# Routed attention and gated FFN on one core: q and k of six pairs cast over 128 partitions and moved by shifts, one output buffer less, a new order

## The chip, the cores and the metric

The kernel runs on one core of one Trainium2 chip. The time is the device time of one execution in microseconds (us); less is better. The kernel before was run three times: 248.41 us in the median, 248.40 to 248.58 from the fastest to the slowest.

A core has five engines that the text names as the profile does: PE (TensorE, matrix products, with its weight loads as PEld), DVE (VectorE), ACT (ScalarE), POOL (GpSimd) and SP (SyncE, which here only issues transfers). Each runs its own list of instructions strictly in order and waits where something it needs is not there yet.

## The reference, cut to what matters

```python
# q, k, v: 4 batches x 8 heads x 768 tokens x 64
q_assign = argmax(q_n @ c_n.T)               # nearest of 16 centroids, k likewise
mask = q_assign[:, :, :, None] == k_assign[:, :, None, :]
scores = where(mask, (q @ k.T) / 8, -1e9)
attn = exp(scores) / sum(exp(scores))
x = (attn @ v), heads side by side           # 4 x 768 x 512
h = relu(x @ w_in)                           # 512 -> 1024
conv = 3-tap filter along the tokens of h, per channel
out = (h * sigmoid(conv)) @ w_out            # 1024 -> 512
```

## The kernel before

**Work units.** Two heads of one batch are a pair; there are 16 pairs, 0 to 15, four per batch. For each pair the scores are made in the transposed form for half of the queries at a time, so there are 32 attention units t = 0 to 31: batch b = t // 8, half t % 8 // 4, pair 4b + t % 4. The feed-forward part has 8 units per batch (n = 0 to 31: two 128-channel blocks of the 1024, for half of the tokens).

**The path of a pair.** SP loads q, k and v (`load`, L243; `load_v`). Pairs 0 to 9 are transposed on PE (step T) and copied out of PSUM by DVE or ACT (Qd, Qa). Pairs 10 to 15 are loaded in 32x32 blocks by eight transfers (LQ.g.0 to .3, LK.g.0 to .3) and transposed in place on DVE (step D, `block_transpose`, L285). Both give `qkT`, a tile of 128 partitions (head 0 on partitions 0 to 63, head 1 on 64 to 127) by q and k. From it

- PE makes the similarities with the centroids (A, L302), DVE finds each token's centroid in seven steps M0 to M6 (L315) and packs it as three rows, PE turns them (K, L371), DVE or ACT copies them (Bd, Ba) and SP moves them into `ext` (BX, L381);
- q and k are cast to f16 into rows 0 to 63 of `ext`, one head at a time, in four instructions of 64x768 (CD with the engine's letter p, d or a, then the pair, head, and q or k; `cast_direct`, L288).

`ext` has five buffers, and holds q and k with the bias rows in rows 64 to 66, so that one product gives scores and mask together. v is cast by CV.

**Attention and the rest.** For each unit t: six score steps S.t.0 to S.t.5 (PE, L401), each followed by an exponential E (ACT, L413), values V (PE, L432), then NR and N on DVE (L443, L448: reciprocal of the sums, normalization). x is transposed by PE (X, with a copy Y) or by a transfer (XD), goes through I (PE, L486), a relu (Ra on ACT, Rd on DVE), filter taps on DVE (cw, aw, bw for whole units, c, a, b for halves, L518 and L520), tanh on ACT (H, L548) and the gate on DVE (G, L557). The output product is in steps O.b.tq.i of two matmuls each (L569); Fa or Fd copies a finished tile out of PSUM into `o_sb`, and FX stores it.

**What sets the order.** One string of steps, `PLAN`, is walked from left to right (`step`, L721) and each step appends its instructions to its engines' lists. Nothing reorders them later. `BUFS` gives the number of buffers of each rotating tile: writing into one whose last reader is not done makes the engine wait. Steps for another path of the casts are in the code, and no step of the order before calls them:

```python
def cast_direct(name, g, h, o):
    copy(name, ext_b[g % NE][0:D, h, o], qkT[g][D * h : D * (h + 1), o, :])

def cast_qk(name, g, o):
    if g not in c_t:
        c_t[g] = rot.tile([P, 2, S], F16, name="c16", tag="c16", bufs=BUFS["c16"])
    copy(name, c_t[g][:, o], qkT[g][:, o])

def shift_qk(g, h):
    nc.sync.dma_start(ext_b[g % NE][0:D, h], c_t[g][D * h : D * (h + 1)])
```

Of the kernel before, what the change touches and what calls it, by code (L numbers as in the profile page):

```python
# [19 lines left out]
BUFS = {'qk_in': 4, 'qkT': 2, 'c16': 2, 'v_in': 2, 'spk': 2, 'attn': 4, 'x16': 3, 'cnv': 2, 'th': 2, 'hg': 2, 'o_sb': 3, 'w_sb': 1, 'sim': 1, 'eqq': 1, 'val': 1, 'mx': 3, 'best': 3, 'rec': 3}  # L20

PLAN = (
# [123 lines left out]
def kernel(  # L146
# [91 lines left out]
    def qk_in(g):  # L238
        if g not in qk_t:
            qk_t[g] = rot.tile([P, 2, 2 * J * D], F32, name="qk_in", tag="qk_in", bufs=BUFS["qk_in"])  # L240
        return qk_t[g]
# [598 lines left out]
```

## Time and profile before

| | |
|---|---|
| median of 3 runs | 248.41 us |
| the profiled execution | 248.59 us |
| its span in the profile | 246.4 us |
| busy: PE, DVE, ACT, POOL | 232.0, 225.2, 212.7, 77.4 us |
| transfers | 32.07 MB, 130 GB/s in the mean |
| TensorE clock granted | 1.00 throughout |

The span reaches from the first to the last instruction of the program; 2.2 us of the execution lie around it. All durations are from this one execution. Matmuls are pipelined, so that one of 162 ns behind another shows as about 325 ns: PE's busy time says when PE has work, not that it works at its peak. An idle time is put down to what ended it.

### The profile page before, as it was taken

How to read it: one execution, taken by the hardware profiler on the slowest of the kernel's cores; microseconds unless marked ns; L12 is line 12 of the kernel's file. 1: busy time of each engine (PE TensorE's matmuls, PEld its weight loads, DVE VectorE, ACT ScalarE, POOL GpSimd, SP SyncE). 2: the span in 40 equal slices, each digit the busy share in tenths (PEclk: the TensorE clock that was granted, in tenths of full speed). 3: DMA queues.
4: the chain of work that ended last, by engine and by line, in shares of the span. 5: the costliest groups of instructions: out<-in, count | busy, mean ns of one | idle time of the engine just before them, and what ended most of it. 6: DMA issues, size and time to landing. Idle time of an engine off the chain costs nothing.

```text
span 246.4 us, 6267 instructions
## 1 busy us (share of the span) xinstructions
PE 232.0 (94%) x2447; PEld 148.2 (60%) x2447; DVE 225.2 (91%) x434; ACT 212.7 (86%) x331; POOL 77.4 (31%) x122
## 2 busy tenths in 40 slices
PE   8898999999999998798999999979999999999994
PEld 8675677666746674555455566645566666665541
DVE  6689867997999999999999999999999999999962
ACT  2578999997999999889899999979999999996730
POOL 6372681786162209346300615221500000000000
PEclk9999999999999999999999999999999999999999
DMA  8968999793480934646277984868300450002424
GB/s 160 220 158 212 262 211 327 217 287 83 124 193 13 203 56 82 126 80 122 45 131 159 232 74 122 153 86 135 84 19 6 124 182 0 3 1 109 150 85 170
DMA packets 95561, 32.07 MB, mean 130 GB/s; under 512 B 88361, under 2 KB 90921, under 8 KB 95532
## 3 DMA queue, kind: packets, MB, share of 16 engines
q1 hardware_dynamic: 93820, 31.25, 55.6%
q10 hardware_dynamic: 1712, 0.43, 1.0%
q8 instruction: 19, 0.31, 0.5%
q14 instruction: 10, 0.08, 0.1%
HBM read 23.11 MB, written 6.29 MB: 119 GB/s over the span
## 4 chain that ended last, share of the span: by engine, by line
PE 48%; DVE 33%; ACT 9%; issue 5%; DMA 3%; SPq 1%; POOL 0%; DVEq 0%; POOLq 0%; ACTq 0%
PE sc L401 13%; PE flex L569 9%; PE flex L432 7%; DVE cnv L520 6%; PE flex L486 5%; DVE hg L557 4%; PE flex L306 3%; ACT attn L413 3%; DMA xT<-x 3%; PE tail L569 3%; PE flex L278 3%; DVE eqq L339 3%; DVE x L448 2%; PE tail L486 2%; DVE cnv L518 2%
## 5 line engine op out<-in xcount | busy, mean ns | idle before, releaser
L413 ACT ACTIVATE attn<-sc 128x768 f16<-128x768 f32 x192 | 147.6, 830 | 6.2 <-PE sc L401 5.1
L401 PE MATMUL sc<-ext 128*128 128x384 f16 x384 | 90.8, 325 | 1.4 <-ACT attn L413 0.9
L236 POOL CAST ext<-qkT 64x768 f16<-64x768 f32 x44 | 44.0, 1008 | 72.4 <-DVE qkT L286 30.2
L520 DVE SCALAR_TENSOR_TENSOR cnv<-hpad,cwcol,cnv 128x768 f16<-128x768 f16 (+2 forms) x72 | 64.1, 904 | 0.2
L432 PEld LDWEIGHTS <-attn 128*128 128x128 f16 x1152 | 51.1, 97 | 18.7 <-issue 3.1
L432 PE MATMUL flex<-v,attn 128*128 128x65 f16 x1152 | 55.0, 193 | 0.1
L401 PEld LDWEIGHTS <-ext 128*128 128x128 f16 x384 | 31.6, 97 | 24.9 <-issue 10.9
L486 PE MATMUL flex<-xT,w_in 128*128 128x384 f16 x224 | 44.8, 325 | 1.0 <-DVE x L448 0.7
L569 PE MATMUL flex<-w_out,hg 128*128 128x512 f16 x160 | 43.7, 379 | 1.0 <-DVE x L448 1.0
L486 PEld LDWEIGHTS <-w_in 128*128 128x128 f16 x256 | 24.2, 97 | 17.1 <-issue 1.6
L557 DVE SCALAR_TENSOR_TENSOR hg<-th,hpad 128x768 f16<-128x768 f32 (+3 forms) x34 | 31.8, 944 | 0.5 <-ACT th L548 0.3
L548 ACT ACTIVATE th<-cnv 128x768 f32<-128x768 f16 (+2 forms) x30 | 26.1, 871 | 2.0 <-DVE cnv L520 1.8
L569 PEld LDWEIGHTS <-hg 128*128 128x128 f16 x192 | 17.5, 97 | 15.7 <-issue 1.4
L499 ACT ACTIVATE hpad<-flex 128x384 f16<-128x384 f32 x40 | 20.1, 518 | 0.2
L278 PE MATMUL flex<-id,qk_in 128*128 128x128 f32 x120 | 17.8, 277 | 1.9 <-DVE nrm_c L662 0.8
L448 DVE TENSOR_TENSOR x<-flex,rec 128x384 f16<-128x384 f32 x32 | 17.5, 546 | 0.5 <-DVE rec L443 0.3
L236 POOL CAST v<-v_in 128x768 f16<-128x768 f32 x12 | 11.3, 938 | 18.7 <-DMA v_in<-in_v_dram 10.4
L278 PEld LDWEIGHTS flex<-id,qk_in 128*128 128x128 f32 x120 | 13.5, 142 | 5.1 <-DVE nrm_c L662 1.0
L518 DVE TENSOR_SCALAR cnv<-hpad,cwcol 128x768 f16<-128x768 f16 (+2 forms) x36 | 15.4, 434 | 0.5 <-ACT hpad L499 0.3
L306 PE MATMUL flex<-qkT,cT 128*32 128x384 f32 x128 | 13.6, 498 | 0.5 <-DVE hpad L501 0.4
L234 ACT ACTIVATE qkT<-flex 128x512 f32<-128x512 f32 x15 | 8.8, 602 | 5.4 <-PE flex L278 5.4
L330 DVE STREAM_TRANSPOSE sim<-flex 128x384 f32<-128x384 f32 x16 | 9.2, 578 | 4.0 <-PE flex L306 3.6
(82 smaller groups left out, 223.1 us busy)
## 6 DMA issues: line engine op xcount, KB each, us to landing
v_in<-in_v_dram SPq DMA_DIRECT2D x16, 384.0 KB
out_dram<-o_sb SPq DMA_DIRECT2D x9, 512.0 KB
qk_in<-in_q_dram SPq DMA_DIRECT2D x20, 192.0 KB
qk_in<-in_k_dram SPq DMA_DIRECT2D x9, 384.0 KB
qk_in<-in_q_dram SPq DMA_DIRECT2D x24, 96.0 KB
qk_in<-in_k_dram SPq DMA_DIRECT2D x24, 96.0 KB
w_sb<-in_moe_w_in_dram SPq DMA_DIRECT2D x4, 512.0 KB
w_sb<-in_moe_w_out_dram SPq DMA_DIRECT2D x4, 512.0 KB
```

The source lines that it names most:

```text
L236: (nc.vector if name == "d" else nc.gpsimd).tensor_copy(out=to, in_=src)
L278: nc.tensor.transpose(bank[at][:, P * i : P * (i + 1)], qk_t[g][:, o, P * j : P * (j + 1)], id128[:])
L306: nc.tensor.matmul(bank[at][32 * j : 32 * (j + 1), 0:HS], lhsT=cT32[:, g % NPR, :], rhs=tokens[:, j], start=True, stop=True, skip_group_ch ...
L401: nc.tensor.matmul(s[:, n, 0:HS], lhsT=ext_b[g % NE][:, h, 1, P * (kt + n) : P * (kt + n + 1)], rhs=ext_b[g % NE][:, h, 0, HS * a : HS * ( ...
L413: nc.scalar.activation(attn[t, i // 3][:, kt : kt + 2, :], sc[(6 * t + i) % 2][:, :, 0:HS], AF.Exp, scale=0.125)
L432: nc.tensor.matmul(avp(at)[:, u, 0 : D + 1], lhsT=attn[t, h][:, kt, P * jq : P * (jq + 1)], rhs=v16_b[g % NE][:, h, kt, 0 : D + 1], start= ...
L448: nc.vector.tensor_tensor(out=x16[t].rearrange("p jq (h d) -> p h jq d", h=2), in0=av[:, :, 0:D].rearrange("p (h jq) d -> p h jq d", h=2), ...
L486: nc.tensor.matmul(bank[at][:, 0:HS], lhsT=w_in16[:, r, 2 * u + f, :], rhs=xT[:, b % 2, r, HS * a : HS * (a + 1)], start=(r == 0), stop=(r ...
L520: nc.vector.scalar_tensor_tensor(out=cnv, in0=src, scalar=w, in1=cnv, op0=ALU.mult, op1=ALU.add)
L548: nc.scalar.activation(th, cnv_t[key].rearrange("p (f s) -> p f s", s=N), AF.Tanh, scale=0.5)
L557: nc.vector.scalar_tensor_tensor(out=hg_b[b][:, 2 * u + fs.start : 2 * u + fs.stop, lo : lo + N], in0=th, scalar=1.0, in1=hpad(b, u)[:, fs ...
L569: nc.tensor.matmul(bank[at][:, 0:Dm], lhsT=hg_b[b][:, fb, P * tq : P * (tq + 1)], rhs=w_out16[:, fb, :], start=(fb == 0), stop=(fb == NFB ...
```

## The change

In the code two numbers and the string of steps change.

```diff
-BUFS = {'qk_in': 4, 'qkT': 2, 'c16': 2, 'v_in': 2, ..., 'o_sb': 3, 'w_sb': 1, ...}
+BUFS = {'qk_in': 4, 'qkT': 2, 'c16': 1, 'v_in': 2, ..., 'o_sb': 2, 'w_sb': 1, ...}
 PLAN = (
...
-    "S.17.5 I.14.0@0 cw.1.1.0 M2.11 aw.1.1.0 Fa.0.4 E.17.5 I.14.1@1 Ra.14.1 Hw.1.0.0 BX.10 LV.12 I.12.1@2 "
+    "CQp.11.1 aw.1.0.0 M2.11 bw.1.0.0 V.16.1@0 V.16.2@0 I.14.0@3 Ra.14.0 S.17.3 E.17.3 S.17.4 I.13.0@1 Ra.13.0 "
...
```

For pairs 10 to 15 the four casts CD are replaced by two steps CQ (`cast_qk`: q or k of both heads at once, 128x768, into a tile `c16`) and two steps CX (`shift_qk`: a transfer on SP's queue that moves one head's 64 partitions of q and k, 64x1536 f16, from `c16` to rows 0 to 63 of `ext`). Eleven CQ are on POOL and one, CQd.15.0, on DVE. `c16` has one buffer, so that a pair's CQ waits until both shifts of the pair before it have landed. `o_sb` has two buffers instead of three.

The rest of the string is a new order of the same steps, with other engines for some of them (counts before and after):

| step | before | after |
|---|---|---|
| casts CD on POOL, DVE, ACT | 44, 12, 8 | 25, 10, 5 |
| casts CQ on POOL, DVE | 0, 0 | 11, 1 |
| shifts CX | 0 | 12 |
| casts of v on POOL, DVE, ACT | 12, 3, 1 | 15, 0, 1 |
| bias copies on DVE, ACT | 13, 5 | 9, 9 |
| chunk copies of q and k on DVE, ACT | 15, 15 | 13, 17 |
| output evacuations on DVE, ACT | 8, 16 | 3, 21 |

Three places of the order. The first is DVE's list in the first 17 us, from the first head's last argmax steps of pair 0 to the second head's (`hpack0` holds the packed rows of pair 0, `hpack1` those of pair 1, `sim` the similarities of a pair). Before:

```order
L333 TENSOR_REDUCE mx_267<-sim_243 128x12
L236 COPY spk_324<-flex1_67 36x128
L339 TENSOR_TENSOR eqq_326<-sim_243,mx_267 128x192
L330 STREAM_TRANSPOSE sim_328<-flex2_68 128x384
L345 TENSOR_TENSOR val_330<-eqq_326,iota16_83 128x192
L333 TENSOR_REDUCE mx_332<-sim_328 128x12
L349 TENSOR_REDUCE best_334<-val_330 128x12
L339 TENSOR_TENSOR eqq_337<-sim_328,mx_332 128x192
L353 TENSOR_SCALAR hpack0_108<-best_334 128x12
L333 TENSOR_REDUCE mx_340<-sim_328 128x12
L369 TENSOR_TENSOR hpack0_108<-hpack0_108 128x2x6
```

And now, at the same place:

```order
L339 TENSOR_TENSOR eqq_304<-sim_242,mx_277 128x192
L236 COPY spk_323<-flex1_67 36x128
L345 TENSOR_TENSOR val_325<-eqq_304,iota16_83 128x192
L349 TENSOR_REDUCE best_327<-val_325 128x12
L353 TENSOR_SCALAR hpack0_108<-best_327 128x12
L369 TENSOR_TENSOR hpack0_108<-hpack0_108 128x2x6
L330 STREAM_TRANSPOSE sim_338<-flex0_66 128x384
L333 TENSOR_REDUCE mx_390<-sim_338 128x12
```

The steps of pair 1 (those on the second `sim`) no longer stand between pair 0's.

The second place is SP's list around the bias rows of pairs 14 and 15 (`spk` to `ext4` and `ext0`), some 175 to 190 us into the span before. Before:

```order
L470 DMA_TRANSPOSE xT_80<-x16_2948 128x3x128
L265 DMA v_in_3008<-in_v_dram 128x12x64
L384 DMA ext4_99<-spk_3060 3x24x128
L470 DMA_TRANSPOSE xT_80<-x16_3097 128x3x128
L384 DMA ext0_95<-spk_3165 3x24x128
L470 DMA_TRANSPOSE xT_80<-x16_3221 128x3x128
```

And now:

```order
L470 DMA_TRANSPOSE xT_80<-x16_2824 128x3x128
L593 DMA out_0_dram<-o_sb_2948 128x2x512
L297 DMA ext4_99<-c16_3053 64x1536
L384 DMA ext4_99<-spk_3048 3x24x128
L297 DMA ext4_99<-c16_3053 64x1536
L265 DMA v_in_3102<-in_v_dram 128x12x64
L297 DMA ext0_95<-c16_3099 64x1536
L384 DMA ext0_95<-spk_3097 3x24x128
L297 DMA ext0_95<-c16_3099 64x1536
L470 DMA_TRANSPOSE xT_80<-x16_3042 128x3x128
```

The four shifts stand around the bias rows, and a store of an output tile and the load of pair 15's v are now among them.

The third place is DVE's list at the same time, where `pack0` gets the last rows of pair 15's argmax and `spk` is the copy of its turned rows. Before:

```order
L365 TENSOR_TENSOR pack0_105<-pack0_105 128x2x2x6
L520 SCALAR_TENSOR_TENSOR cnv_3099<-hpad2_112,cwcol_86,cnv_3099 128x768
L518 TENSOR_SCALAR cnv_3163<-hpad3_113,cwcol_86 128x768
L236 COPY spk_3165<-flex2_68 72x128
L520 SCALAR_TENSOR_TENSOR cnv_3099<-hpad2_112,cwcol_86,cnv_3099 128x768
```

And now:

```order
L365 TENSOR_TENSOR pack0_105<-pack0_105 128x2x2x6
L520 SCALAR_TENSOR_TENSOR cnv_3065<-hpad2_112,cwcol_86,cnv_3065 128x768 x2
L236 COPY spk_3097<-flex2_68 72x128
L236 CAST c16_3099<-qkT_2956 128x768
L520 SCALAR_TENSOR_TENSOR cnv_3073<-hpad2_112,cwcol_86,cnv_3073 128x768 x2
```

The cast into `c16`, which waits for the shifts of pair 14, stands behind the copy and ahead of two filter taps.

More of the change, by code (lines that the diff above doesn't have):

```diff
@@ L19 @@
 NHK = 2
-BUFS = {'qk_in': 4, 'qkT': 2, 'c16': 2, 'v_in': 2, 'spk': 2, 'attn': 4, 'x16': 3, 'cnv': 2, 'th': 2, 'hg': 2, 'o_sb': 3, 'w_sb': 1, 'sim': 1, 'eqq': 1, 'val': 1, 'mx': 3, 'best': 3, 'rec': 3}
+BUFS = {'qk_in': 4, 'qkT': 2, 'c16': 1, 'v_in': 2, 'spk': 2, 'attn': 4, 'x16': 3, 'cnv': 2, 'th': 2, 'hg': 2, 'o_sb': 2, 'w_sb': 1, 'sim': 1, 'eqq': 1, 'val': 1, 'mx': 3, 'best': 3, 'rec': 3}
 PLAN = (
[119 rows of a table removed]
[119 rows of a table added]
 )
```

236 rows, old and new, of the table PLAN are left out of this document.

## The prediction

> **What bounds the kernel now.** I read four views in this order: busy time by stage, the chain that ended last, the groups of instructions with their shapes, and the timelines around a few waits. By stage first (columns: stage and its length, then busy time of PE, PE's weight loads, DVE, ACT and POOL with instruction counts, granted clock, DMA share):
>
> ```profile
> 21.00:60.00 39.00, 37.76 (x476) 26.44 (x477) 32.11 (x70) 36.14 (x53) 23.89 (x38) 1.00 0.83 233
> 60.00:105.00 45.00, 41.95 (x489) 28.22 (x488) 44.09 (x85) 43.07 (x67) 17.77 (x21) 1.00 0.55 117
> 105.00:168.00 63.00, 59.60 (x619) 35.31 (x615) 62.74 (x106) 58.77 (x92) 20.37 (x18) 1.00 0.68 122
> 168.00:220.00 52.00, 52.00 (x545) 32.11 (x542) 50.76 (x93) 51.14 (x81) 4.32 (x5) 1.00 0.25 61
> ```
>
> The limit changes hands. From 60 to 168 us DVE is never free (44.09 of 45, 62.74 of 63), while ACT has 1.9 and 4.2 us of room there and PE 3.1 and 3.4. From 168 us PE is without a gap (52.00 of 52). The chain that ended last agrees: it runs on DVE up to about 166 us and then on PE to the end.
>
> ```profile
> 235.86 6.92 PE tail L569 x32
> 242.78 0.02 issue
> 242.81 0.60 ACT o_sb L584
> ```
>
> So a microsecond counts in two ways: as DVE time before 168 us, and as matmul work left over after it.
>
> **The change part by part: casts and copies on DVE.** I count steps of the order by name, on DVE, between two steps that stand in both orders: M0.8 (the first argmax step of pair 8, 80 us before) and M0.14 (that of pair 14, 171 us before). Their counts: casts of q or k straight into ext (CDd) from 2 to 0, the cast of v (CVd) from 1 to 0, copies of bias rows (Bd) from 4 to 2; one normalization (NR and N) is moved in from behind. All else on DVE is equal in number. The one cast of the new kind that DVE gets (CQd.15.0) stands behind M0.14. Durations (minimum/median/maximum in ns, first for POOL, then DVE):
>
> ```profile
> L236 POOL CAST ext<-qkT x44: 816/824/1633, 9.1 to 176.0; 64x768 f16<-64x768 f32 x44
> ...
> L236 DVE COPY spk<-flex x13: 179/210/228, 13.7 to 184.5; 72x128 f16<-72x128 f16 x11, 36x128 f16<-36x128 f16 x2
> L236 POOL CAST v<-v_in x12: 822/842/1261, 17.6 to 159.3; 128x768 f16<-128x768 f32 x12
> L236 DVE CAST ext<-qkT x12: 542/554/1293, 19.7 to 170.8; 64x768 f16<-64x768 f32 x12
> ...
> L236 DVE CAST v<-v_in x3: 547/548/559, 67.0 to 181.6; 128x768 f16<-128x768 f32 x3
> ```
>
> The normalization that comes in (mean ns of one after the comma):
>
> ```profile
> L448 DVE TENSOR_TENSOR x<-flex,rec 128x384 f16<-128x384 f32 x32 | 17.5, 546 | 0.5 <-DVE rec L443 0.3
> ...
> L443 DVE RECIPROCAL rec<-flex 128x6 f32<-128x6 f32 x32 | 5.9, 183 | 1.1 <-PE flex L432 1.1
> ```
>
> 2 x 0.554 + 0.548 + 2 x 0.210 - 0.546 - 0.183 = **1.35 us** less for DVE in the stretch that it bounds. If the moved normalization is not charged it is 2.08. Further back five output evacuations leave DVE on balance, four of them in the last 10 us, where DVE waits for PE: nothing.
>
> **POOL.** For pairs 10 to 15 POOL had 19 casts of q or k and 3 of v; it now has 11 and 5. A cast over 128 partitions costs what one over 64 does (842 against 824 ns above), so that is six casts less, 22 to 16. POOL itself has room everywhere. What counts is that a DVE instruction running beside it is stretched. DVE's three long kinds from 105 to 180 us, with 23 POOL instructions (18 and 5 in the table by stage), and from 180 to 214 us, with none:
>
> ```profile
> L520 DVE SCALAR_TENSOR_TENSOR cnv<-hpad,cwcol,cnv 128x768 f16<-128x768 f16 x21 | 23.0, 1100 | 0.0
> L557 DVE SCALAR_TENSOR_TENSOR hg<-th,hpad 128x768 f16<-128x768 f32 x12 | 12.1, 1018 | 0.0
> ...
> L518 DVE TENSOR_SCALAR cnv<-hpad,cwcol 128x768 f16<-128x768 f16 x10 | 5.1, 514 | 0.2 <-ACT hpad L499 0.2
> ```
>
> ```profile
> L520 DVE SCALAR_TENSOR_TENSOR cnv<-hpad,cwcol,cnv 128x768 f16<-128x768 f16 x15 | 15.1, 1009 | 0.1
> L557 DVE SCALAR_TENSOR_TENSOR hg<-th,hpad 128x768 f16<-128x768 f32 x8 | 7.5, 947 | 0.0
> ...
> L518 DVE TENSOR_SCALAR cnv<-hpad,cwcol 128x768 f16<-128x768 f16 x7 | 2.8, 407 | 0.2 <-ACT hpad L499 0.2
> ```
>
> 21 x 0.091 + 12 x 0.071 + 10 x 0.107 = 3.83 us of stretch from 23 instructions; six fewer save 3.83 x 6/23 = **1.0 us**. Bounds: 0, if the casts that stay are those that collide, and 2.0, if the six that go cost twice the mean. The Trainium skill, page SBUF — State Buffer, section Who interferes with whom, says that a DVE instruction with two SBUF inputs or in a two-port mode and a GpSimd instruction lock each other out of a shared port pair for a whole instruction; by that rule six casts less could give back up to 6 x 0.84 = 5.0 us, where the rows give 1.0. On a single collision the trace agrees: the longest DVE cast took 1293 against 554 ns.
>
> **PE.** Behind S.24.0 (168 us before), where PE takes over, the new order has 68 steps of the output product (O) against 66; all other PE work behind it is equal. One step is two matmuls, 2 x 6.92/32 = 0.43 us by the chain above, so **0.86 us** more are left to do when PE becomes the limit.
>
> **Start.** The first score matmul waits for a small transfer:
>
> ```profile
> 19.89 0.27 PE L374 MATMUL flex<-id,hpack 128*128 128x128 f16 x2 [0.28 <-DVE hpack L369]
> 20.00 0.60 PE L278 MATMUL flex<-id,qk_in 128*128 128x128 f32 x4
> 21.01 0.48 PE L401 MATMUL sc<-ext 128*128 128x384 f16 x2 [0.40 <-DMA ext<-spk]
> ```
>
> The new order puts the other head's argmax steps later on DVE and sends these rows ahead of the next loads, so that wait should go. What is late next is the turn of the second pair at 19.89, which still stands ahead on PE: at most 21.01 - 20.16 = 0.85 us won. But three more copies of q and k are put on ACT before 62 us, and ACT is the fullest engine after PE there (36.14 of 39). I take 0 for both, with 0.85 either way.
>
> **The new wait.** Twelve transfers of 64x1536 f16 (192 KB) are new, on SP's queue. For pair 15 there is a chain: with a single c16 buffer, DVE's cast CQd.15.0 waits until the second shift of pair 14 (CX.14.1) has landed, and the shift CX.15.0, ahead of which S.27.0 may not start, waits for that cast. Queued behind the cast on DVE are the next two filter taps; behind S.27.0 on PE is everything. On SP each shift also waits for its pair's casts, and a few loads of the next pair stand behind it; those loads are asked for a whole pair later, so I put 0 on that. The trace has no such transfer. Its nearest rows are a 9 KB one (issued at 18.34, ended the wait at 21.01: 2.67 us), a 384 KB one (19.17 to 22.41: 3.24 us) and a transposing one behind a row of loads:
>
> ```profile
> 18.34 0.79 SPq L386 DMA_DIRECT2D ext<-spk  x1
> 19.17 0.43 SPq L267 DMA_DIRECT2D v_in<-in_v_dram  x1
> ```
>
> ```profile
> 22.41 1.01 POOL L236 CAST v<-v_in 128x768 f16<-128x768 f32 x1 [3.82 <-DMA v_in<-in_v_dram]
> ```
>
> ```profile
> 140.39 4.75 DMA xT<-x
> ```
>
> I take d = 3.0 us, between the first two by size, and keep 2.67 and 4.75. The time that is there, from SP's and PE's timelines:
>
> ```profile
> 179.11 0.76 SPq L384 DMA_DIRECT2D ext<-spk  x1
> ```
>
> ```profile
> 181.92 0.48 PE L401 MATMUL sc<-ext 128*128 128x384 f16 x2
> ...
> 187.32 0.49 PE L401 MATMUL sc<-ext 128*128 128x384 f16 x2
> ```
>
> From the issue of pair 14's bias rows (179.11) to S.27.0 (187.32) are 8.21 us. In the new order 0.76 for that issue, d for CX.14.1, 0.55 for the cast and d for CX.15.0 must fit: 1.31 + 2d = 7.3 us. It fits with 0.9 us to spare: **0**. At d = 4.75 it is 10.8, a stall of 2.6 us on the engine that sets the end. A rule speaks against these transfers: the Trainium skill, page SBUF — State Buffer, section on the DMA port swizzle, says that partitions 0 to 63 reach half of the ports, 196 GB/s measured, and the next section that about 2 us are fixed. By that page my estimate is 2.0 + 1.0 = 3.0 us, and the sum would be the same; no run here shows it yet.
>
> **One output buffer less:** 0. The last evacuation now needs the store of the one two before it to have landed; eight O steps, 3.46 us, lie between their matmuls, and from the last evacuation's end (243.41) to the end of the span (246.4), a store included, are 2.99 us.
>
> **Sum.** 1.35 + 1.0 - 0.86 = 1.5 us less. ACT's 4.2 and PE's 3.4 us of room in the stage from 105 to 168 us cover the 2.35 that DVE gives up. The profiled execution took 248.59 us (a span of 246.4 and 2.2 around it), 0.18 over the median of 248.41. 248.59 - 1.5 - 0.18 = **246.9 us**.
>
> **Rivals.**
> *A, slower: the shifts land late.* With d at 4.75 the chain of pair 15 stalls PE by 2.6 us: 246.9 + 2.6 = 249.5. It decides from the point where the stall eats the gain of 1.5: 1.31 + 2d = 9.7, d = 4.2. For it: the 4.75 row, and that a store of an output tile now stands just ahead of CX.14.0 on SP. Against: the DMA share is 0.25 from 168 to 220 us, against 0.68 where 4.75 was seen. Chance 0.20.
> *B, nothing won: DVE is freed, but another order of ACT or PE work stalls in its place.* For it: three engines are within 7% of full from 105 to 168 us, so small misfits cost. Then 248.4. Chance 0.17, a quarter of it beyond 0.2% on the slow side.
> *C, more won.* The start gives its 0.85 and the collisions 2.0: 246.9 - 0.85 - 1.0 = 245.0. Chance 0.17.
> The forecast keeps 0.46.
>
> **How the numbers follow.** About 0.2%, 0.5 us, is what a measurement of this kernel can tell from no change. Faster: 0.46 + 0.17 = 0.63; same: three quarters of B, 0.13; slower: 0.20 + 0.04 = 0.24. The range goes from C's 245.0 to A's 249.5, where a stall at the longest transfer shown ends.
>
> **What would show it.** Right: DVE busy 1 to 2.5 us less before S.24.0, that score step 2 to 2.5 us earlier than 168.0, the three stretched kinds nearer to 1009, 947 and 407 ns, PE without a gap from there, and shifts landing in about 3 us. Wrong: PE waiting for the shift before S.26.0 or S.27.0 (A), or S.24.0 no earlier with idle time on ACT or PE before it (B).

## The result and the profile after

The changed kernel takes 244.93 us (244.74 to 245.0, 4 runs) against 248.50 us (248.40 to 248.64, 4 runs) of the kernel before: a ratio of 0.9846, 95% interval 0.9813 to 0.9878, 3.6 us less. The forecast was 246.9, with a range of 245.0 to 249.5, so its direction was right, and the gain is more than twice as large. The profiled execution took 245.0 us, with a span of 243.2 us and the clock at 1.00.

Busy time by stage, with the stages of the prediction (PE, PE's weight loads, DVE, ACT, POOL, then clock, DMA share, GB/s):

```profile
21.00:60.00 39.00, 37.87 (x470) 26.42 (x469) 31.81 (x70) 37.05 (x55) 24.28 (x39) 1.00 0.81 228
60.00:105.00 45.00, 42.90 (x505) 29.52 (x504) 43.00 (x86) 42.92 (x66) 17.68 (x20) 1.00 0.53 121
105.00:168.00 63.00, 62.36 (x653) 37.33 (x650) 60.83 (x106) 60.65 (x97) 14.29 (x14) 1.00 0.79 149
168.00:220.00 52.00, 51.77 (x539) 32.01 (x536) 50.56 (x93) 48.83 (x78) 3.69 (x4) 1.00 0.31 82
```

Read PE's column first. PE's work is the same in both kernels, 232.0 us of busy time, so the span falls by the idle time that PE loses: 246.4 - 232.0 = 14.4 us before, 243.2 - 232.0 = 11.2 us now. Stage by stage it is 1.24 to 1.13, 3.05 to 2.10, 3.40 to 0.64, and 0.00 to 0.23 us. From 60 to 168 us 3.7 us of idle time are gone, and behind that a little comes back. DVE, which was busy 62.74 of 63 us, is now at 60.83.

The waits of PE for one cause, from 60 to 168 us (line, what it waited for: total, times, longest). Before:

```profile
PE flex L374 <- DVE x L448: 1.5, 1, 1.5
PE flex L569 <- DVE x L448: 1.0, 2, 0.7
PE flex L374 <- DVE hpad L501: 1.0, 1, 1.0
PE flex L486 <- DVE x L448: 0.7, 1, 0.7
```

After, the whole list:

```profile
PE flex L374 <- DVE pack L365: 1.3, 1, 1.3
PE sc L401 <- ACT attn L413: 1.2, 4, 0.4
```

Of PE's waits for DVE these four rows, 4.2 us together, have become one of 1.3 us. S.24.0, before and after:

```profile
168.04 0.48 PE L401 MATMUL sc<-ext 128*128 128x384 f16 x2
```

```profile
163.33 0.49 PE L401 MATMUL sc<-ext 128*128 128x384 f16 x2
```

That is 4.7 us earlier, where the prediction had 2 to 2.5. Of these, 0.98 us are there at M0.8 already, which starts at 78.62 us instead of 79.60, and for which the prediction had nothing: from 60 to 79 us PE's idle time falls from 0.70 us to 0. And the DVE instructions that POOL stretches, from 105 to 180 us (16 POOL instructions start in it, 23 before). Three of the kinds stand in the prediction; four more of before:

```profile
L286 DVE STREAM_TRANSPOSE qkT<-qk_in 128x768 f32<-128x768 f32 x12 | 11.5, 966 | 0.0
L448 DVE TENSOR_TENSOR x<-flex,rec 128x384 f16<-128x384 f32 x11 | 6.0, 544 | 0.1
...
L339 DVE TENSOR_TENSOR eqq<-sim,mx 128x384 f16<-128x384 f32 x6 | 3.8, 638 | 0.0
...
L345 DVE TENSOR_TENSOR val<-eqq,iota 128x384 f16<-128x384 f16 x6 | 2.6, 436 | 0.0
```

and after:

```profile
L520 DVE SCALAR_TENSOR_TENSOR cnv<-hpad,cwcol,cnv 128x768 f16<-128x768 f16 x23 | 23.5, 1025 | 0.2
L286 DVE STREAM_TRANSPOSE qkT<-qk_in 128x768 f32<-128x768 f32 x12 | 11.4, 960 | 0.0
L557 DVE SCALAR_TENSOR_TENSOR hg<-th,hpad 128x768 f16<-128x768 f32 x11 | 10.4, 957 | 0.3 <-ACT th L548 0.3
L448 DVE TENSOR_TENSOR x<-flex,rec 128x384 f16<-128x384 f32 x11 | 6.0, 548 | 0.1
L518 DVE TENSOR_SCALAR cnv<-hpad,cwcol 128x768 f16<-128x768 f16 x11 | 4.5, 410 | 0.3 <-ACT th L548 0.3
...
L339 DVE TENSOR_TENSOR eqq<-sim,mx 128x384 f16<-128x384 f32 x6 | 3.3, 552 | 0.0
...
L345 DVE TENSOR_TENSOR val<-eqq,iota 128x384 f16<-128x384 f16 x6 | 2.0, 340 | 0.0
```

The means of L520, L557 and L518 were 1100, 1018 and 514 ns; they are now almost those of a stage without POOL (1009, 947, 407). Of the 3.83 us of stretch 23 x 0.016 + 11 x 0.010 + 11 x 0.003 = 0.5 us are left.

The whole stretch of the program in which the prediction counted, from M0.8 to M0.14, before and after:

```profile
79.60:171.34 91.74, 85.98 (x938) 52.73 (x937) 91.03 (x157) 86.27 (x132) 31.35 (x31) 1.00 0.66 121
```

```profile
78.62:168.25 89.63, 86.90 (x955) 54.14 (x954) 86.60 (x153) 85.90 (x134) 25.76 (x28) 1.00 0.72 139
```

DVE has three instructions less to do there (the rows say four, since one at the edge of the first window is counted with it) and is busy 4.43 us less, and the stretch is 2.11 us shorter, while PE does 0.92 us more in it.

The shifts (KB each, us from issue to landing), and the chain of pair 15, which the prediction feared most (SP's queue, then POOL, DVE and PE):

```profile
ext<-c SPq DMA_DIRECT2D x12, 192.0 KB, 3.4
```

```profile
176.08 0.51 SPq L297 DMA_DIRECT2D ext<-c  x1
...
180.62 0.48 SPq L297 DMA_DIRECT2D ext<-c  x1
181.56 0.79 SPq L384 DMA_DIRECT2D ext<-spk  x1
```

```profile
178.94 1.11 POOL L236 CAST c<-qkT 128x768 f16<-128x768 f32 x1 [9.97 <-DMA ext<-c]
```

```profile
179.42 1.05 DVE L236 CAST c<-qkT 128x768 f16<-128x768 f32 x1
```

```profile
184.23 0.48 PE L401 MATMUL sc<-ext 128*128 128x384 f16 x2 [0.17 <-ACT th L548]
```

The first row knows the landing of one shift only; by the semaphore events in the trace all twelve took 2.72 to 5.08 us, 3.42 in the median. CX.14.1 is issued at 176.08 and has landed at 178.80, which releases POOL's CQp.15.1 at 178.94. DVE's CQd.15.0 has no idle time ahead of it, but takes 1.05 us beside POOL's cast, where the prediction had 0.55. CX.15.0 is issued at 180.62 and has landed at 183.35, ahead of S.27.0 at 184.23. The profile puts the 0.17 us of idle time there down to ACT's tanh, which S.27.0 does not use. The bias rows of pair 15, which it does use, are issued behind CX.15.0 at 181.56 and have landed at 184.10, about when the tanh ends (184.09), so the wait is more likely theirs. The new wait costs at most these 0.17 us.

### The profile page after: what moved, and what is told of

Read it like the earlier page. It is cut to its first block, busy times and chain, and to the rows that moved or that the text cites. A ratio compares the mean times of both kernels' runs of the same rounds, so it can differ in the third digit from the quotient of the medians.

```text
span 243.2 us, 6281 instructions
## 1 busy us (share of the span) xinstructions
PE 232.0 (95%) x2447; PEld 149.6 (61%) x2447; DVE 215.3 (89%) x423; ACT 213.8 (88%) x337; POOL 70.9 (29%) x115
## 4 chain that ended last, share of the span: by engine, by line
PE 79%; DVE 8%; ACT 7%; DMA 2%; issue 2%; POOL 1%; ACTq 0%; DVEq 0%
PE sc L401 21%; PE flex L569 13%; PE flex L486 13%; PE flex L432 12%; PE flex L278 5%; PE flex L306 5%; ACT attn L413 4%; PE tail L569 3%; PE sc L644 3%; PE tail L486 2%; DMA ext<-spk 2%; DVE cnv L520 1%; DVE hg L557 1%; ACT qkT L234 1%; DVE x L448 1%
## 5 line engine op out<-in xcount | busy, mean ns | idle before, releaser
L520 DVE SCALAR_TENSOR_TENSOR cnv<-hpad,cwcol,cnv 128x768 f16<-128x768 f16 (+2 forms) x72 | 63.5, 895 | 0.4
L432 PEld LDWEIGHTS <-attn 128*128 128x128 f16 x1152 | 51.9, 97 | 19.2 <-issue 3.3
L432 PE MATMUL flex<-v,attn 128*128 128x65 f16 x1152 | 56.2, 193 | 0.6 <-DVE hpad L501 0.6
L486 PE MATMUL flex<-xT,w_in 128*128 128x384 f16 x228 | 45.2, 325 | 0.1
L569 PE MATMUL flex<-w_out,hg 128*128 128x512 f16 x160 | 42.6, 379 | 0.0
L486 PEld LDWEIGHTS <-w_in 128*128 128x128 f16 x256 | 24.1, 97 | 16.6 <-issue 0.5
L557 DVE SCALAR_TENSOR_TENSOR hg<-th,hpad 128x768 f16<-128x768 f32 (+3 forms) x34 | 30.7, 913 | 0.8 <-ACT th L548 0.3
L236 POOL CAST ext<-qkT 64x768 f16<-64x768 f32 x25 | 22.7, 920 | 26.2 <-ACT qkT L234 20.2
L236 POOL CAST c<-qkT 128x768 f16<-128x768 f32 x11 | 11.9, 1083 | 54.0 <-DVE qkT L286 22.7
L499 ACT ACTIVATE hpad<-flex 128x384 f16<-128x384 f32 x41 | 20.9, 531 | 0.2
L236 POOL CAST v<-v_in 128x768 f16<-128x768 f32 x15 | 13.9, 926 | 18.8 <-DMA v_in<-in_v_dram 13.1
L278 PE MATMUL flex<-id,qk_in 128*128 128x128 f32 x120 | 17.3, 280 | 0.0
L278 PEld LDWEIGHTS flex<-id,qk_in 128*128 128x128 f32 x120 | 13.9, 144 | 2.2 <-DVE val L345 0.6
L518 DVE TENSOR_SCALAR cnv<-hpad,cwcol 128x768 f16<-128x768 f16 (+2 forms) x36 | 14.1, 394 | 0.4 <-ACT th L548 0.3
```

What stands on the lines that cost most here:

```text
L236: (nc.vector if name == "d" else nc.gpsimd).tensor_copy(out=to, in_=src)
L278: nc.tensor.transpose(bank[at][:, P * i : P * (i + 1)], qk_t[g][:, o, P * j : P * (j + 1)], id128[:])
L432: nc.tensor.matmul(avp(at)[:, u, 0 : D + 1], lhsT=attn[t, h][:, kt, P * jq : P * (jq + 1)], rhs=v16_b[g % NE][:, h, kt, 0 : D + 1], start= ...
L486: nc.tensor.matmul(bank[at][:, 0:HS], lhsT=w_in16[:, r, 2 * u + f, :], rhs=xT[:, b % 2, r, HS * a : HS * (a + 1)], start=(r == 0), stop=(r ...
L499: nc.scalar.activation(to, src, AF.Relu)
L520: nc.vector.scalar_tensor_tensor(out=cnv, in0=src, scalar=w, in1=cnv, op0=ALU.mult, op1=ALU.add)
```

## The experiments

Theory 1: the gain is the casts, fewer on POOL, which therefore holds DVE up less. Theory 2: the gain is the new order. There are twelve runs, two of them (e5 and e11) of the changed kernel itself. The kernel before was timed beside them (medians 248.18 us for e1 to e4, 248.54 for e5 to e8, 248.76 for e9 to e11, 248.78 for e12). The ratios are to that; they and their 95% intervals are estimated from all the executions, so a ratio can differ a little from that of two medians. In e1 to e4 and e6 to e9 the line numbers are one or two higher than in the text. Where a run needs `c16` beside three output buffers, the tile lies in the buffer of the weights' staging tile:

```diff
-c_t[g] = rot.tile([P, 2, S], F16, name="c16", tag="c16", ...)
+c_t[g] = rot.tile([P, 2, 1024], F16, name="c16", tag="w_sb", ...)[:, :, 0:S]
```

**e1, the casts alone, in the old order.** Here for pair 12; pairs 10 to 15 alike.

```diff
-CDp.12.0.1 CDp.12.1.1 CDp.12.0.0 CDp.12.1.0
+CQp.12.1 CQp.12.0 ... CX.12.0 CX.12.1
```

> The order before, with only the casts of pairs 10 to 15 changed in place: twelve casts over 128 partitions, all on GpSimd (POOL), and twelve shifts; GpSimd has 15 casts for these pairs instead of 22, VectorE (DVE) two fewer, ScalarE (ACT) three fewer. Theory 1 (the gain is the smaller number of casts): DVE is stretched in proportion, 3.83 x 15/22 = 2.6 instead of 3.8 us in its three long kinds, loses 1.1 us of casts as well, and the time falls by 2 to 3 us, to 245.5 to 246.5. Theory 2 (the gain is the new order, which lays the casts of GpSimd beside DVE instructions that they do not hold up): still some ten stretched DVE instructions from 105 to 180 us, and at most 1 us won, 247.5 to 248.5.

Measured: 247.49 us against 248.18, 0.9965 (0.9945 to 0.9985). Too little for theory 1, but PE shows a wait that is new (in the profiled execution, the slowest of twelve at 248.70 us):

```profile
137.45 0.50 PE L402 MATMUL sc<-ext 128*128 128x384 f16 x2 [1.69 <-DMA ext<-spk]
```

S.19.0 waits for the bias rows of pair 11: the two shifts of pair 11 had been put on SP's queue ahead of the loads of pair 12 and a store of 512 KB, so that those 18 KB were issued 0.55 us later than before (133.96 against 133.41). S.19.0 started 2.64 us after their issue before (136.05), and 3.49 us after it here. So this run mixes the casts' gain with the price of a badly placed shift. Run e9 takes them apart.

**e2, the new order alone.**

```diff
-CQp.12.1 ... CQp.12.0 CX.12.0 ... CX.12.1
+CDp.12.0.1 CDp.12.1.1 ... CDp.12.0.0 CDp.12.1.0
```

> The changed kernel with its new order and two output buffers, but each cast over 128 partitions made again as two casts of 64 partitions straight into ext on the same engine, one behind the other, and no shifts: GpSimd has 22 casts where the changed kernel has 11. Theory 1 (number of casts): most of the gain is lost, 247 to 248.5, DVE stretched as in the kernel before. Theory 2 (place of the casts): the gain stays, 244.9 to 246, although each doubled cast reaches into the next DVE instruction; DVE's stretched instructions from 105 to 180 us fewer than the 14 of before.

Measured: 247.10 us, 0.9955 (0.9938 to 0.9971). As theory 1 had it, at the low end of its 247 to 248.5: 2.5 of the 3.6 us are lost. But 1.1 us stay, which fewer casts on POOL cannot explain. This kernel has the counted change too: the casts and copies of the 1.35 us are off DVE in it. DVE's stretch is back with the 11 additional casts:

```profile
L558 DVE SCALAR_TENSOR_TENSOR hg<-th,hpad 128x768 f16<-128x768 f32 x11 | 11.5, 1057 | 0.0
L519 DVE TENSOR_SCALAR cnv<-hpad,cwcol 128x768 f16<-128x768 f16 x11 | 5.6, 506 | 0.0
```

(the lines 557 and 518 of the changed kernel, 957 and 410 ns there).

**e3, three output buffers again.**

```diff
-'o_sb': 2
+'o_sb': 3
```

`c16` lies in the staging tile's buffer, of which there is one.

> The changed kernel with three output buffers again; the room comes from putting the c16 tile where the weights' staging tile lies, which is not used after 70 us. As forecast (the buffer costs nothing): 244.9 within 0.3, the last 25 us the same. Rival (the two buffers cost the 0.4 us by which PE's idle time behind 220 us grew, 3.63 to 4.01): 244.5.

Measured: 246.26 us, 0.9912 (0.9887 to 0.9937), against 0.9863 (0.9837 to 0.9888) for the changed kernel itself (e5). The third buffer wins nothing in sum, but the run does not show that the second costs nothing. Between PE's last product and the last evacuation there are 0.37 us in the changed kernel, 0.34 of them idle time for which the profile names no cause; here they are 0.07, as the kernel before has 0.03. Runs e2, e5, e10 and e11, with two buffers, have the 0.3 us too. So the missing buffer costs about 0.3 us at the very end, probably the wait for the store that the prediction named. Why this run is slower even so is not settled. Its profile has one new wait of PE, 0.4 us for a transposing transfer, and 3.69 us from the end of the last evacuation to the end of the span, against 3.05.

**e4, the kernel before with short casts.** This kernel leaves out 704 of the 768 columns of the 19 casts of q and k that POOL does for pairs 10 to 15.

```diff
-copy(name, ext_b[g % NE][0:D, h, o], qkT[g][D * h : D * (h + 1), o, :])
+n = 64 if g >= 10 and name == "p" else S
+copy(name, ext_b[g % NE][0:D, h, o, :n], qkT[g][D * h : D * (h + 1), o, :n])
```

> The kernel before, with the 19 casts of q and k of pairs 10 to 15 on GpSimd cut from 768 to 64 columns: the other columns are left out, so these pairs' scores use old values; the order and all waits stay. Theory of the stretch (what GpSimd does to DVE is what the change takes away): DVE's three long kinds from 105 to 180 us come down to about 1010, 950 and 410 ns, DVE's busy time there falls by 4 to 5 us, and the time by 2 to 3.5 us, to 245 to 246.5, where PE becomes the limit. Rival (the stretch is hidden and the order of PE's work is what won): DVE's busy time falls as well, but the time stays within 0.7 us of 248.5.

Measured: 246.57 us, 0.9932 (0.9906 to 0.9958), 1.6 us less with order and work as before. From M0.8 to M0.14:

```profile
79.53:168.97 89.44, 86.00 (x938) 52.92 (x937) 87.87 (x157) 86.10 (x132) 23.96 (x31) 1.00 0.66 124
```

The same 157 DVE instructions as before take 3.2 us less, and 2.3 us of that reach M0.14. POOL's casts do hold the kernel before up, by way of DVE. The 1.6 us are less than the 2 to 3.5 expected, though more than the 0.7 of the rival, and DVE lost 3.2 us, not 4 to 5. The expectation on the means was only nearly met: 1023, 981 and 463 ns, since POOL's casts of v and one of pair 9 still run there.

**e5, the changed kernel again; e6, each POOL cast into c16 twice.**

```diff
-copy(name, c_t[g][:, o], qkT[g][:, o])
+for _ in range(1 + (name == "p")):
+    copy(name, c_t[g][:, o], qkT[g][:, o])
```

> The changed kernel itself again, on the chip of the next three and beside the kernel before: 0.985 of its time, as at first, within 0.3%. It is what the next three are compared with.

> The changed kernel with each of GpSimd's eleven casts into c16 made twice, one behind the other; nothing else is changed. Theory of the stretch: GpSimd reaches into the next DVE instruction, DVE's busy time from 105 to 180 us grows by 11 x 0.17 to 11 x 0.35 = 1.9 to 3.9 us; DVE has 2.2 us idle from 105 to 168 us, so the time grows by 0 to 2 us. Rival (the stretch is not what sets the time any more, only the shifts that start 0.8 us later): DVE's busy time grows as well, and the time by less than 0.4 us.

Measured: e5 245.22 us, 0.9863 (0.9837 to 0.9888), as in the result above. e6 247.70 us, 0.9967 (0.9948 to 0.9985): 2.5 us more than e5, above the 0 to 2 expected. So 11 casts cost 2.5 us, 0.23 us each; e2 gives about the same with the same number of casts and no shifts, so the shifts have no part in it. From M0.8 to M0.14:

```profile
78.16:170.37 92.21, 88.12 (x955) 53.89 (x954) 89.64 (x154) 86.21 (x134) 33.90 (x35) 1.00 0.70 135
```

DVE has 3.0 us more than in the changed kernel, and the stretch is 2.6 us longer. That DVE had 2.2 idle us from 105 to 168 us did not help.

**e7, the first scores earlier.**

```diff
-K.1.1@0 K.1.0@2 BX.0.1 LK.3 BX.0.0 ... Ba.1.1 Ba.1.0 S.0.0 T.3.2@3 S.0.1 E.0.0
+BX.0.1 LK.3 BX.0.0 ... S.0.0 S.0.1 E.0.0 K.1.1@0 K.1.0@2 Ba.1.1 Ba.1.0 T.3.2@3
```

> The changed kernel with the second pair's turns (the two K.1 steps) and their copies put behind the first two score steps and the first exponential: the first score then waits only for the transfer of pair 0's bias rows, which in the changed kernel landed at 19.4 us, 1.35 us ahead of the first score at 20.76. Theory that PE's idle time is what is left to win: the first score at about 19.5 us, and 0.5 to 1.2 us less time. Rival (ACT, busy 37.05 of 39 us from 21 to 60 us, sets the pace there): the gain is gone by 60 us, and the time stays within 0.3 us.

Measured: 247.96 us in the median, but ten of the twelve executions ran at a lower granted clock (last section). The two at 1.00 took 245.45 and 245.63 us, against 245.22 of the changed kernel (e5): nothing is won. The profile is of one of these two. Two rows of PE:

```profile
19.50 0.82 PE L402 MATMUL sc<-ext 128*128 128x384 f16 x4 [0.15 <-POOL ext L237]
...
31.44 0.50 PE L402 MATMUL sc<-ext 128*128 128x384 f16 x2 [1.40 <-DMA ext<-spk]
```

and the second place in the changed kernel:

```profile
31.27 0.50 PE L401 MATMUL sc<-ext 128*128 128x384 f16 x2 [0.39 <-DMA ext<-spk]
```

The first score comes 1.26 us earlier, and all of it is gone at S.2.0, which waits for pair 2's bias rows and starts 0.17 us later than without the edit. Not ACT, as the rival had it, but the next transfer.

**e8, more work for DVE.** D.12.1 and D.13.0 are made twice:

```diff
-nc.vector.transpose(qkT_of(g)[:, o, :], qk_t[g][:, o, :])
+for _ in range(1 + ((g, o) in ((12, 1), (13, 0)))):
+    nc.vector.transpose(qkT_of(g)[:, o, :], qk_t[g][:, o, :])
```

> The changed kernel with two of DVE's block transposes made twice (q or k of pairs 12 and 13, 128x768, 0.96 us each, between 130 and 145 us): 1.9 us more work for DVE, none for another engine. If PE bounds the changed kernel from 105 us on, as its 62.36 busy of 63 us say, DVE's 2.2 idle us take it up and the time grows by 0 to 0.5 us. If DVE still bounds it, by 1.9 us.

Measured: 247.23 us, 0.9945 (0.9921 to 0.9969), 2.0 us above e5. From M0.8 to M0.14:

```profile
79.26:170.64 91.38, 86.95 (x955) 54.07 (x954) 88.66 (x156) 85.86 (x134) 25.66 (x28) 1.00 0.71 137
```

DVE 2.06 us more, the length 1.75. This is the 1.9 us expected if DVE still bounds the changed kernel, not the 0 to 0.5 if PE does. How 1.9 us on DVE reach PE past 2.2 idle us shows in three timelines. DVE:

```profile
144.52 2.81 DVE L288 STREAM_TRANSPOSE qkT<-qk_in 128x768 f32<-128x768 f32 x3
147.25 0.67 DVE L347 TENSOR_TENSOR val<-eqq,iota 128x384 f16<-128x384 f16 x1
147.85 1.57 DVE L522 SCALAR_TENSOR_TENSOR cnv<-hpad,cwcol,cnv 128x768 f16<-128x768 f16 x1
```

ACT:

```profile
149.45 0.84 ACT L550 ACTIVATE th<-cnv 128x768 f32<-128x768 f16 x1 [1.60 <-DVE cnv L522]
150.20 2.19 ACT L415 ACTIVATE attn<-sc 128x768 f16<-128x768 f32 x3
```

PE:

```profile
151.04 0.49 PE L403 MATMUL sc<-ext 128*128 128x384 f16 x2 [1.67 <-ACT attn L415]
```

The filter tap ends late (it also takes 1.57 us, against 1.01 in the changed kernel, so a part of the delay is a new collision). ACT's tanh waits for it 1.60 us, the exponentials queued behind the tanh are late, and the next score waits for their buffer 1.67 us. DVE's idle time lies at other places, where DVE waits for PE or ACT; it does not take up work that comes elsewhere.

**e9, the casts alone with better placed shifts.**

```diff
-BX.10 LV.12 CX.11.0 CX.11.1 LQ.12.1 ... LQ.12.2 FX.0.0 LK.12.2 LK.12.3 BX.11
+BX.10 LV.12 LQ.12.1 ... LQ.12.2 CX.11.0 CX.11.1 LK.12.2 LK.12.3 BX.11 FX.0.0
```

> Run e1 again (the order before, only the casts of pairs 10 to 15 changed), with one difference on SyncE's queue: the two shifts of pair 11 stand behind the loads of pair 12, and the 512 KB store of the first output tiles is moved from ahead of pair 11's bias rows to behind them. In e1 those bias rows landed late and S.19.0 waited 1.69 us for them. If that wait is why e1 won only 0.7 to 0.9 us, S.19.0 waits for less than 0.5 us and the time is 1.8 to 2.5 us below the kernel before. Rival (the casts in the old order are worth no more, because GpSimd's casts still lie beside DVE's filter taps): 0.7 to 1.2 us below it.

Measured: 247.05 us against 248.76, 0.9919 (0.9892 to 0.9946), 1.7 us less, and no wait of S.19.0 in the list of PE's waits. Theory 1, a little below the range expected: in the old order the casts are worth 1.7 us, and the place of two shifts and of one store about 1.0 of it. Of the 3.83 us of stretch, by the means of the three kinds here (1057, 961 and 466 ns), 22 x 0.048 + 12 x 0.014 + 10 x 0.059 = 1.8 us are left. With e2, order and casts multiply to 0.9919 x 0.9955 = 0.987, the changed kernel's 0.985 to 0.986 within the intervals. That does not show that the two gains are independent, since both runs take the two casts CDd off DVE.

**e10, pairs 8 and 9 too; e11, the changed kernel beside it.**

```diff
-CDp.8.1.0 CDp.8.1.1 CVp.8 _wp.8 CDp.8.0.1 CDp.8.0.0 ... XD.10
+CQp.8.0 CQp.8.1 CVp.8 _wp.8 ... CX.8.0 CX.8.1 XD.10
...
-CDp.9.0.0 CDp.9.1.0 CDp.9.1.1 CVp.9 CDp.9.0.1 ... XD.12
+CQp.9.0 CQp.9.1 CVp.9 ... CX.9.0 CX.9.1 XD.12
```

> The changed kernel with pairs 8 and 9 cast in the same way: four casts over 128 partitions instead of eight of 64 and four more shifts, ahead of the transfers of x of units 10 and 12. From 80 to 105 us DVE had 6 instructions beside GpSimd that were stretched by 2.4 us together. If the price of a cast is 0.2 us as e2 and e6 show, four fewer save 0.8 us: 0.4 to 1.2 us below the changed kernel in the same call. Rival (the remaining casts run over other taps, or the shifts hold back pair 8's or 10's transfers): within 0.3 us of it, or slower.

> The changed kernel once more, on the chip of the two others: 0.985 to 0.987 of the kernel before.

Measured: e10 243.28 us, 0.9784 (0.976 to 0.9809); e11 245.00, 0.985 (0.9826 to 0.9874). Another 1.7 us less, more than expected, and the fastest version. From 78 to 105 us two DVE kinds of the changed kernel were

```profile
L520 DVE SCALAR_TENSOR_TENSOR cnv<-hpad,cwcol,cnv 128x768 f16<-128x768 f16 x8 | 8.4, 1066 | 0.0
...
L339 DVE TENSOR_TENSOR eqq<-sim,mx 128x384 f16<-128x384 f32 x2 | 2.3, 1126 | 0.0
```

and are now

```profile
L520 DVE SCALAR_TENSOR_TENSOR cnv<-hpad,cwcol,cnv 128x768 f16<-128x768 f16 x9 | 9.0, 1004 | 0.0
...
L339 DVE TENSOR_TENSOR eqq<-sim,mx 128x384 f16<-128x384 f32 x2 | 1.4, 681 | 0.0
```

8 x 0.062 + 2 x 0.445 = 1.4 us of DVE's time are saved in these two, and PE's one long wait for DVE in the changed kernel, the 1.3 us at L374, is no longer in the list of its waits. The prices of e2 and e6 are means again; why more was won than they say was not taken further apart.

**e12, pair 7 too.**

```diff
-CDp.7.0.1 ... CDa.7.1.1 ... CDd.7.0.0 CDp.7.1.0
+CQp.7.0 CQp.7.1 ... CX.7.0 CX.7.1
```

> Run e10 with pair 7 cast in the same way too: its four casts of 64 partitions on GpSimd (two), DVE and ACT, near 69 us, become two over 128 partitions on GpSimd, and two shifts go out on SyncE's queue near 70 us, which has nothing to issue from 70 to 78 us. DVE (1.06 us) and ACT (0.83) lose a cast each in a stage in which ACT and DVE are both within 2 us of full. If three engines that wait for each other in turn set the pace there, the kernel takes 0.3 to 0.9 us less than e10's 0.978 of the kernel before: 0.975 to 0.977. Rival (nothing waits on these casts, or the shifts land behind loads of 384 KB and S.11.0 waits): 0.978 or more.

Measured: 244.49 us, 0.9826 (0.98 to 0.9851): not better than e10, probably worse, as the rival had it. In its profile the transpose of pair 8 on PE waits 0.85 us for ACT, where e10 has no gap. But the profiled execution was the slowest of seven (246.70 us; the others took 243.59 to 244.80), and S.2.0 starts 1.36 us later in it than in e10, far ahead of the edit. Why one cast fewer on ACT and DVE wins nothing stays open.

## Why the prediction was wrong

Its direction and its mechanism held. The step that failed is the size of the POOL term, 1.0 us. Beside it, a gain that the order brings ahead of M0.8 was put at nothing.

- **What bounds the kernel.** DVE ahead of 168 us was right (e4, e8). Taking the 3.1 and 3.4 us of PE's room there as cover, not as what could be won, was the blind spot: PE's waits for DVE in that room are where most of the gain came from.
- **Casts and copies on DVE, 1.35 us.** Three DVE instructions fewer between M0.8 and M0.14, as counted. Of the 4.43 us that DVE's busy time lost between these two steps, 1.35 are the count at the prediction's prices and about 3.1 the stretch.
- **POOL, 1.0 us, between 0 and 2.0: the step that failed.** "Six fewer save 3.83 x 6/23" took a mean price for each cast. Measured are the 3.1 us of DVE's time, above the upper bound too; in the time of the kernel they are 2.3 (see the order). Kind by kind, 3.3 of the 3.83 us in the three kinds are gone, and in the argmax kinds L339 and L345, which the step left out, 6 x 0.086 + 6 x 0.096 = 1.1 us. These means add up to more than 3.1, since they go by fixed times with other steps in them, and records of neighbours on DVE overlap a little. Even in the old order (e9), with 15 casts for 22, 2.0 of the 3.83 went, more than a mean price gives. With the new order, most of the casts that stayed ceased to collide too (the eleven into `c16` take 830 ns in the median, the longest still 1595): a price belongs to a pair of instructions and not to a cast. Before, POOL's chain of four casts runs over two taps:

```profile
137.39 5.29 POOL L236 CAST ext<-qkT 64x768 f16<-64x768 f32 x4 [13.95 <-DVE qkT L286]
```

```profile
140.02 0.48 DVE L518 TENSOR_SCALAR cnv<-hpad,cwcol 128x768 f16<-128x768 f16 x1
140.42 1.57 DVE L520 SCALAR_TENSOR_TENSOR cnv<-hpad,cwcol,cnv 128x768 f16<-128x768 f16 x1
```

  After, the two casts of the same pair lie beside a transpose, an evacuation and a normalization, and neither side is stretched (1.70 us for two casts; 0.92 and 0.53 us as elsewhere):

```profile
134.62 1.70 POOL L236 CAST c<-qkT 128x768 f16<-128x768 f32 x2 [1.82 <-DVE rec L443]
```

```profile
134.51 0.92 DVE L286 STREAM_TRANSPOSE qkT<-qk_in 128x768 f32<-128x768 f32 x1
135.36 0.65 DVE L586 TENSOR_SCALAR o_sb<-flex 128x512 f32<-128x512 f32 x1
135.94 0.53 DVE L448 TENSOR_TENSOR x<-flex,rec 128x384 f16<-128x384 f32 x1
```

  Over 105 to 180 us the transposes L286 took 966 ns before and 960 after, the normalizations 544 and 548, while the taps went from 1100 to 1025: some kinds are held up, others are not. The Trainium skill, page SBUF — State Buffer, section Who interferes with whom, says just that: DVE instructions with one SBUF input outside the two-port modes, and reductions, do not contend with GpSimd. The up to 5.0 us that the prediction worked out by that section lie about as far above the 3.1 measured as the 1.0 from the rows lies below.
- **The order, 0.** The prediction counted what the new order moves and gave its own gaps no value. e2 shows 1.1 us for the new order, with the four waits of PE for DVE shown above gone from its list too. But e2 contains the 1.35 us of casts and copies, so the 1.1 do not come on top of them. By parts, e2 has M0.8 1.15 us earlier than before (78.45); from M0.8 to S.24.0 (165.50) it is 1.39 us shorter, about what the count had; behind S.24.0 it loses 1.4. From M0.8 to S.24.0 the changed kernel is 2.34 us shorter still, and that is what its fewer casts are worth in time. So what the working put at nothing is about 1 us ahead of M0.8. Two waits of PE for DVE, of 0.4 and 0.2 us at L278 and L486 between 60 and 79 us, are gone there in e2 and in the changed kernel; which of the moved steps does it was not tried.
- **PE, 0.86 us more behind S.24.0.** Right for the work: PE is busy 75.63 us from there on, 74.73 before. But the whole stretch from S.24.0 to the end of the span grew by 1.5 us, from 78.4 to 79.9, because of idle time that the prediction put at nothing (0.23 from 168 to 220, 0.38 behind; the points on the shifts and on the output buffer say where most of it may come from).
- **Start, 0.** Right up to 60 us: the first score 0.25 us earlier (20.76), S.2.0 0.30 us later (31.27 against 30.97). e7 shows that even 1.26 us there would be lost at the next transfer.
- **The new wait and the shifts, 0 with d = 3.0.** Nearly right: pair 15's chain fits, and costs at most 0.17 us. The median shift took 3.4 us, but the two on the chain 2.7, which made up for a cast of 1.05 us where 0.55 was reckoned. One shift off the chain, CX.14.0, took 5.08, more than the 4.75 of rival A. The prediction's estimate of 3.0 us by the Trainium skill (the same page, the section on the DMA port swizzle) is 0.4 short of the median. That a shift can cost elsewhere shows e1: on a queue in order its price is paid by the small transfer behind it.
- **The output buffer, 0.** Not quite: about 0.3 us at the end (e3).
- **The rivals.** C, "more won", named the right mechanism and a time of 245.0, which is what came, but this is luck: half of its extra came from a start that gave nothing, and its collisions, 2.0, were a third smaller than measured. Neither A, but for the 0.17 us at S.27.0, nor B took place.

In sum, at the prediction's own boundaries: M0.8 is 0.98 us earlier, where 0 was forecast; from M0.8 to S.24.0 the kernel is 3.73 us shorter, where 2.35 were forecast; and 1.5 us were given back behind S.24.0, where 0.86 were forecast. That makes the 3.2 us of the span. Not all of what DVE loses is time: in e4, e6 and e8 2.3 of 3.2, 2.6 of 3.0 and 1.75 of 2.06 us of a change of its busy time showed in the length of the stretch.

## What to carry to other kernels

Price a GpSimd instruction by the VectorE instruction it will lie beside, not by a mean: making 24 casts into 12 paid 1.7 us here in the old order, and with a new order that lays most of them beside transposes, reductions and reads from PSUM nearly all of the stretch went (0.5 of 3.83 us are left). Where three engines are each over 95% busy and feed each other through lists in order, ask what the engine that ends last loses in waiting, for idle time elsewhere is not slack: 1.9 us of additional VectorE work cost 2.0 although VectorE had 2.2 idle. And when a transfer takes the place of a cast, look at the smallest transfer behind it on the queue.

## What was not expected of the hardware

In e7, 10 of the 12 executions had a granted TensorE clock of 0.984 to 0.993 in the mean and took 247.2 to 249.7 us; the two at 1.000 took 245.45 and 245.63. The changed kernel, which differs from it only in the place of a few steps near 20 us, was at 0.998 to 1.000 in the five executions timed beside it (e5). Whether that edit is the cause, and by what, was not tried.
